# Rows of w and u spread by shuffles, quartered weights and new planner durations in a fused RWKV-5 and feed-forward kernel

## The chip, the cores and the metric

The kernel runs on one core of a Trainium2 chip. The core has a matrix engine (PE, with its weight loads PEld), a vector engine (DVE), a scalar engine (ACT), a general engine (POOL) and a synchronising engine (SP), each with its own in-order instruction queue, and 16 DMA engines which all queues share. The metric is device time in microseconds of one execution.

## The reference

For each of 4 batches and 8 heads (768 steps, head size 48) a state of 48 x 48 is carried along the sequence:

```python
for t in range(S):
    cur = np.einsum('bhd,bhe->bhde', u[None] * kt, vt)
    y[:, :, t] = np.einsum('bhd,bhde->bhe', rt, state + cur)
    state = w[None, :, :, None] * state + np.einsum('bhd,bhe->bhde', kt, vt)
```

Then y, as 3072 tokens of 384, goes through a feed-forward part: `h = x @ w_in` (384 to 2048), an elementwise gate (h above 1, 0 below -1, (h+1)^2/4 between), and `g @ w_out` (2048 to 384). All inputs and the output are float32.

## The kernel before, in words

The sequence is cut in chunks of 128 steps, so the recurrence becomes matrix work. A group g is one chunk of two batches; there are 12 groups of two units (one batch's chunk each), and unit n belongs to group n // 2.

For each group the kernel loads R, K and V (384 KB each) from DRAM by SP's queue (lines 239 and 316). Group 0's R and K come in two halves of 192 KB each, here called R0.0, K0.0, R0.1, K0.1 (the second figure is the batch). R is multiplied by Wup and K by Wdn (powers of w by row, lines 258 and 260), giving Rs and Ks; KU = K u and RKU = R KU (lines 262, 264), a sum of RKU by head (line 289) and V2 = V times that sum (line 294) make the u term. For groups 0 to 4 PE transposes Rs and Ks (T, line 340) and ACT or DVE copies them out (TT, line 163); later groups use DMA transposes (RT, KT, line 424). PE makes A (line 351), DVE masks it (AT, line 356), PE makes the state's update Sp (line 363) and Y (lines 373, 378), DVE adds V2 (y, line 385). The state is multiplied by wCm, a power of w spread over a 96-wide block, on POOL (line 398) or, in the first chunk, on DVE (line 395). y is transposed to xT, on PE for the first three groups (X, line 406), by DMA later (line 447).

The feed-forward part takes 256 tokens of a group in four quarters q: mm1 (12 matmuls to hp, line 463), relu and square on ACT (pt and sq, lines 470 and 474), the gate on DVE (gt, line 478), then mm2 (line 497) for each of the two units, whose result ACT copies out (o_sb) and SP stores. mm1 of q needs its part of w_in, mm2 of q its part of w_out. There are two hp buffers and nine gt buffers.

w and u at the start: both are broadcast over 128 partitions by the transfer (lines 81, 82); ACT makes lw = ln w (line 170), Wup and Wdn by exp (lines 173, 176). w_col holds w by column; POOL squares it seven times (line 180) and ACT spreads it into wCm (line 185).

The order of all work is made when the kernel is built, by a list planner (lines 519 to 581). Each operation is declared with `op(name, where, key, fn, needs, makes, uses)`: the engines it may run on with a duration each, a due time (key), what it needs, which buffers it takes and uses. The planner always takes the engine with the earliest possible start and, on it, the operation with the lowest key among those that can start within 0.25 us, and appends its instructions to that engine's queue. The engines then run these queues in order, with semaphores only where data or buffers demand it. A table SHIFT (line 124) moves the due times of kinds of operations and of single groups.

Weights go by POOL's queue in two halves each (lines 201, 205), which also casts them to bfloat16. Two operations make SP's queue wait: a one-element memset on POOL into R of group 1, behind the w_in issues (line 236), and a small transfer out of w_out's first half ahead of R of group 2 (line 238).

Of the kernel before, what the change touches and what calls it, by code (L numbers as in the profile page):

```python
# [22 lines left out]
def kernel(  # L23
# [51 lines left out]

    w_col = const.tile([P, NP], F32, name="w_col")
    nc.vector.memset(w_col, 1.0)
    mark = const.tile([1, 16], BF16, name="mark")
    w_bc = const.tile([P, DM], F32, name="w_bc")
    u_bc = const.tile([P, DM], F32, name="u_bc")  # L80
# [35 lines left out]

    lw = const.tile([P, DM], F32, name="lw")
# [37 lines left out]

    tiles = {}
# [12 lines left out]
    def lw_ln(e):  # L169
        nc.scalar.activation(lw, w_bc, AF.Ln, bias=0.0)  # L170
# [16 lines left out]
    op("w_bc", (("NET", 0.0, 4.4),), -99, None)  # L187
    op("u_bc", (("NET", 0.0, 5.0),), -99, None)
    op("w_col", (("NET", 0.0, 7.2),), -99, None)
    op("lw", (("ACT", 0.6),), -98, lw_ln, ["w_bc"])  # L190
    op("Wup", (("ACT", 2.0),), -97, wup, ["lw"])
    op("Wdn", (("ACT", 0.7),), -96, wdn, ["Wup"])
    op("w_power", (("POOL", 0.9),), -50, w_power, ["w_col"])
    op("wCm", (("ACT", 0.9),), -49, w_spread, ["w_power"])


    NW = 2
    for i in range(NW):
        def w_in_go(e, i=i):
            n = slice(i * DF // NW, (i + 1) * DF // NW)  # L200
            nc.gpsimd.dma_start(out=w_in_sb[:, :, n], in_=w_in_src[:, :, n])

        def w_out_go(e, i=i):
            n = slice(i * nF // NW, (i + 1) * nF // NW)
            nc.gpsimd.dma_start(out=w_out_sb[:, n, :], in_=w_out_src[:, n, :])

        k_in, k_out = -70 + i, -2 + i * 0.1 + shift("w_out", i)
        op(f"w_in{i}!", (("POOL", 0.8),), k_in, w_in_go, [f"w_in{i - 1}!"] if i else ["load K0.1"])
        op(f"w_in{i}", (("DMA", 4.3, 2.0),), k_in, None, [f"w_in{i}!"])
        op(f"w_out{i}!", (("POOL", 0.9),), k_out, w_out_go, ["load R1.0"])  # L210
        op(f"w_out{i}", (("DMA", 5.0, 2.0),), k_out, None, [f"w_out{i}!"])
# [7 lines left out]
    for g in range(nG):  # L219
# [4 lines left out]
        for j0, j1 in parts:  # L224
# [5 lines left out]
            for i, (x, what) in enumerate(((r, "R"), (k, "K"))):  # L230

                def load(e, g=g, j0=j0, j1=j1, x=x, what=what):
                    if j0 == 0:
                        tiles[what, g] = loads.tile([P, UNITS * H, D], F32, name=what, tag=what)
                    if g == 1 and what == "R":
                        nc.gpsimd.memset(tiles[what, g][:1, 0, :1], 0.0)
                    if g == 2 and what == "R":
                        nc.sync.dma_start(out=mark, in_=w_out_sb[:1, 0, :16])
                    nc.sync.dma_start(out=tiles[what, g][:, j0 * H : j1 * H, :], in_=source(x, g, j0, j1))

                op(f"load {what}{tag}", (("DMA", 1.1 * n, 2.0),), tl + i * 0.3, load, [[], ["w_in1!"], ["w_out0"]][g] if g < 3 else [],
# [24 lines left out]
            pool_or_dve = (("POOL", 0.95 * n), ("DVE", 0.65 * n)) if early_g else (("POOL", 0.92 * n),)  # L266
            pool_only = (("POOL", 0.95 * n),)
            first = j0 == 0
            for i, (what, needs) in enumerate(
# [11 lines left out]
                where = pool_or_dve if i < 2 or g in (1, 2) else pool_only  # L281
                if g == 0 and i < 2:
                    where = (("DVE", 0.6),)
# [240 lines left out]
    free = {"POOL": 4.2, "DVE": 3.0}  # L524
    done = {}
    waiting = dict(ops)
    SLACK, HOP = 0.25, 0.06
    log = []
    last_uses = {}
    queue = {}  # L530
# [81 lines left out]
```

## Time and profile before

| | us |
|---|---|
| median of 3 runs | 192.14 (191.78 to 192.76) |
| the profiled execution | 191.3 |
| its span | 189.5 |
| first mm1 matmul | 22.59 |
| issue of w_in halves on POOL | 10.63 and after |
| issue of w_out halves on POOL | 25.69 and 30.32 |
| issue of R of groups 1 and 2 on SP | 16.62 and 33.57 |

The granted PE clock is full throughout. Busy time of an engine counts its instructions' spans, which overlap on PE; a stretch's columns are PE, PEld, DVE, ACT and POOL busy, each with its number of instructions, the granted clock, the DMA engines' mean busy share (which can come out over 1, as packets overlap) and GB/s. In a row of the timeline the first number is the start, the second the duration, and in brackets the idle time of that engine before it and what ended it. In the chain the two numbers are start and duration. In the rows of the DMA queues they are packets, MB and the share of 16 engines' span.

### The profile page before, as it was taken

The page shows a single profiled execution, that of the slowest core. Times are in us where ns is not written, and L with a number is a line of the kernel's source. Part 1 is how long each engine was busy: PE and PEld are TensorE (multiplying, and loading weights), DVE is VectorE, ACT ScalarE, POOL GpSimd, SP SyncE. Part 2 cuts the span into 40 slices and gives each one's busy share as a digit, 9 for nine tenths or more (in the row PEclk, how much of TensorE's full clock was granted, in tenths as well). Part 3 has the DMA queues.
Part 4 walks back from the last instruction along what each step waited for, and adds up shares of the span by engine and source line. Part 5 has one row for each costly group of instructions (what it writes and reads, how often), then busy time and mean ns, then how long its engine had stood idle before and what let it go on. Part 6 is the DMA issues. An engine that isn't in the chain of part 4 may idle for free.

```text
span 189.5 us, 4017 instructions
## 1 busy us (share of the span) xinstructions
PE 160.8 (85%) x1602; PEld 117.8 (62%) x1602; DVE 135.8 (72%) x181; ACT 134.8 (71%) x166; POOL 118.2 (62%) x95
## 2 busy tenths in 40 slices
PE   0214676599979899989999999999999999999992
PEld 0113454467857677667677677677777767777750
DVE  3477419964989999986969869787888876654540
ACT  3334367938856699986898888869798786778741
POOL 5294095029799999999997999799897300000000
PEclk9999999999999999999999999999999999999999
DMA  4979989979997299899997999799798221121112
GB/s 99 167 117 182 223 136 166 189 150 192 226 249 155 70 186 201 174 194 207 173 218 153 206 182 196 162 177 214 151 197 151 66 66 21 42 66 42 42 42 83
DMA packets 103346, 28.11 MB, mean 148 GB/s; under 512 B 97184, under 2 KB 102560, under 8 KB 103328
## 3 DMA queue, kind: packets, MB, share of 16 engines
q1 hardware_dynamic: 100096, 24.32, 62.7%
q0 software_dynamic: 2944, 3.15, 11.1%
q10 hardware_dynamic: 288, 0.39, 1.0%
q8 instruction: 12, 0.20, 0.4%
q14 instruction: 6, 0.05, 0.1%
HBM read 20.84 MB, written 4.72 MB: 135 GB/s over the span
## 4 chain that ended last, share of the span: by engine, by line
PE 55%; POOL 16%; DVE 8%; DMA 7%; ACT 6%; issue 4%; SPq 0%; POOLq 0%
PE op L497 25%; PE hp L463 24%; POOL KU L262 4%; DMA K<-in_k_dram 4%; POOL RKU L264 3%; POOL Ks L260 3%; DVE gt L478 3%; PE A L351 3%; POOL V L294 2%; DMA KT<-Ks 2%; ACT pt L470 2%; DVE AT L356 2%; ACT sq L474 2%; POOL Rs L258 2%; DMA xT<-y 1%
## 5 line engine op out<-in xcount | busy, mean ns | idle before, releaser
L478 DVE SCALAR_TENSOR_TENSOR gt<-sq,hp 128x1024 bf16<-128x1024 f32 x48 | 58.5, 1218 | 28.4 <-ACT sq L474 28.3
L463 PE MATMUL hp<-xT,w_in_sb 128*128 128x256 bf16 x576 | 72.2, 277 | 3.9 <-DVE gt L478 2.3
L497 PE MATMUL op<-w_out_sb,gt 128*128 128x384 bf16 x384 | 71.0, 326 | 1.6 <-DVE gt L478 0.7
L470 ACT ACTIVATE pt<-hp 128x1024 f32<-128x1024 f32 x48 | 49.1, 1023 | 26.2 <-PE hp L463 25.8
L463 PEld LDWEIGHTS <-w_in_sb 128*128 128x128 bf16 x576 | 56.9, 99 | 16.3 <-issue 4.1
L474 ACT ACTIVATE sq<-pt 128x1024 f32<-128x1024 f32 x48 | 50.8, 1058 | 1.2
L497 PEld LDWEIGHTS <-gt 128*128 128x128 bf16 x384 | 34.5, 97 | 22.2 <-issue 1.3
L356 DVE TENSOR_TENSOR AT<-A,umask 128x512 bf16<-128x512 f32 x48 | 30.8, 683 | 2.5 <-PE A L351 2.1
L258 POOL TENSOR_TENSOR Rs<-R,Wup 128x768 bf16<-128x768 f32 x11 | 20.1, 1828 | 17.6 <-DMA R<-in_r_dram 17.6
L262 POOL TENSOR_TENSOR KU<-K,u_bc 128x768 f32<-128x768 f32 (+1 forms) x13 | 23.3, 1790 | 4.2 <-DMA K<-in_k_dram 4.2
L264 POOL TENSOR_TENSOR RKU<-R,KU 128x768 f32<-128x768 f32 (+1 forms) x13 | 22.5, 1732 | 0.5
L398 POOL TENSOR_TENSOR state<-Tm,wCm 128x384 f32<-128x384 f32 x16 | 16.2, 1014 | 2.5 <-DVE Tm L393 2.4
L294 POOL TENSOR_TENSOR V<-V,diag 128x768 f32<-128x768 bf16 x10 | 14.8, 1483 | 4.7 <-DVE diag L289 3.3
L260 POOL TENSOR_TENSOR Ks<-K,Wdn 128x768 bf16<-128x768 f32 x9 | 16.5, 1829 | 0.0
L385 DVE TENSOR_TENSOR y<-Y,V 128x384 bf16<-128x384 f32 x24 | 13.3, 555 | 4.3 <-PE Y L378 3.0
L163 ACT CAST V<-VF 128x768 bf16<-128x768 f32 x12 | 9.9, 828 | 5.6 <-DMA VF<-in_v_dram 5.6
L378 PE MATMUL Y<-V,AT 128*128 128x48 bf16 x192 | 11.9, 186 | 1.9 <-DVE AT L356 1.9
L163 ACT COPY o_sb<-op 128x384 f32<-128x384 f32 x22 | 10.2, 468 | 3.6 <-PE op L497 3.5
L163 ACT CAST state_bf<-state 128x384 bf16<-128x384 f32 x20 | 10.1, 504 | 3.4 <-DVE state L395 2.8
L289 DVE TENSOR_REDUCE diag<-RKU 128x16 f32<-128x768 f32 (+1 forms) x13 | 11.5, 883 | 1.3 <-POOL RKU L264 1.3
L378 PEld LDWEIGHTS <-AT 128*128 128x128 bf16 x192 | 9.8, 98 | 2.9 <-DVE AT L356 2.6
L340 PE MATMUL T<-ident,Rs 128*128 128x128 bf16 x40 | 4.3, 237 | 6.8 <-DVE Rs L258 6.5
(50 smaller groups left out, 106.7 us busy)
## 6 DMA issues: line engine op xcount, KB each, us to landing
VF<-in_v_dram SPq DMA_DIRECT2D x12, 384.0 KB, 4.3
out_dram<-o_sb SPq DMA_DIRECT2D x24, 192.0 KB, 2.3
R<-in_r_dram SPq DMA_DIRECT2D x11, 384.0 KB, 4.6
K<-in_k_dram SPq DMA_DIRECT2D x11, 384.0 KB, 5.9
w_in_sb<-in_moe_w_in_dram POOLq DMA_DIRECT2D x2, 768.0 KB, 9.0
w_out_sb<-in_moe_w_out_dram POOLq DMA_DIRECT2D x2, 768.0 KB, 8.4
R<-in_r_dram SPq DMA_DIRECT2D x2, 192.0 KB, 5.9
K<-in_k_dram SPq DMA_DIRECT2D x2, 192.0 KB, 5.8
```

What stands on the lines that cost most here:

```text
L163: nc.scalar.copy(out, in_) if e == "ACT" else engines[e].tensor_copy(out, in_)
L258: engines[e].tensor_mul(part(R_s)[:, :, :, :D], part(R), rep(Wup, j1 - j0))
L260: engines[e].tensor_mul(part(K_s)[:, :, :, :D], part(K), rep(Wdn, j1 - j0))
L262: engines[e].tensor_mul(part(tiles["KU", g]), part(K), rep(u_row, j1 - j0))
L264: engines[e].tensor_mul(part(tiles["RKU", g]), part(R), part(tiles["KU", g]))
L356: nc.vector.tensor_mul(tiles["AT", n][:, i], tiles["A", n][i], umask.unsqueeze(1).to_broadcast([P, NP, P]))
L378: nc.tensor.matmul(Y[:, 2 * p + i, :], AT[:, i, p, :], V[:, j * H + 2 * p + i, :], start=(c == 0), stop=True, skip_group_check=True,)
L463: nc.tensor.matmul(hp[:, f, :], w_in_sb[:, i, n0 : n0 + P], tiles["xT", g][:, i, :], start=(i == 0), stop=(i == nK - 1), skip_group_check= ...
L470: nc.scalar.activation(tiles["pt", g, q], tiles["hp", g, q], AF.Relu, bias=0.5, scale=0.5)
L474: nc.scalar.activation(tiles["sq", g, q], tiles.pop(("pt", g, q)), AF.Square, bias=0.0)
L478: nc.vector.scalar_tensor_tensor(out=gt, in0=tiles.pop(("sq", g, q)), scalar=1.0, in1=tiles.pop(("hp", g, q)), op0=ALU.min, op1=ALU.max)
L497: nc.tensor.matmul(tiles["op", g, j], tiles["gt", g, q][:, f, j * P : (j + 1) * P], w_out_sb[:, n, :], start=(n == 0), stop=(n == nF - 1),)
```

## The change

- w and u are loaded as four rows each (partitions 0, 32, 64, 96) into tiles set to 1 and 0 before; a shuffle within each 32 partitions on DVE spreads ln w and u.
- The scalar table is loaded as a set with ln alone at the start and as one with exp behind ln.
- w_col comes by ACT's queue; its squarings may be put on DVE.
- Weights go in four quarters each. Quarter 0 of w_in is issued by POOL behind a one-element copy which reads R0.1, quarter 2 behind one of K of group 1; quarter 0 and 2 of w_out behind R and K of group 2.
- The memset into R and the small transfer out of w_out are gone. In the planner, loads of R of groups 1, 2 and 3 are placed after w_in's quarter 1, its quarter 3 and w_out's quarter 3.
- T of the first four units no longer needs A of the unit before.
- Durations in the planner are new, most with a latency of their own; products on POOL and DVE exclude each other in it (PORT); an operation with two possible engines is entered once, with the one that ends first; KU and RKU of group 0 may go to DVE.

```diff
-    nc.scalar.dma_start(out=w_bc, in_=bcast(w))
-    nc.scalar.dma_start(out=u_bc, in_=bcast(u))
+    nc.vector.memset(w_row, 1.0)
+    nc.vector.memset(u_row4, 0.0)
+    nc.scalar.dma_start(out=w_row[0:P:QUAD, :], in_=bcast(w, P // QUAD))
+    nc.scalar.dma_start(out=u_row4[0:P:QUAD, :], in_=bcast(u, P // QUAD))
+    nc.scalar.preload_act_table_set("natural_log")
     for j in range(2):
-        nc.gpsimd.dma_start(out=w_col[j * HP : j * HP + D, :], in_=src)
-    nc.scalar.preload_act_table_set("natural_log_exp_and_others")
+        nc.scalar.dma_start(out=w_col[j * HP : j * HP + D, :], in_=src)
...
+    LOAD_AFTER = {("R", 1): ["w_in1"], ("R", 2): ["w_in3"], ("R", 3): ["w_out3"]}
...
+    def lw_spread(e):
+        nc.vector.stream_shuffle(lw, lw_row, [0] * QUAD)
+    def u_spread(e):
+        nc.vector.stream_shuffle(u_bc, u_row4, [0] * QUAD)
...
+    op("exps", (("ACT", 1.28),), -98, lambda e: nc.scalar.preload_act_table_set("exp_and_others"), ["lw_row"])
-    op("w_power", (("POOL", 0.9),), -50, w_power, ["w_col"])
+    op("w_power", (("DVE", 0.6),), -50, w_power, ["w_col"])
...
-    NW = 2
+    NW = 4
+    GATE_IN = {0: ("R", 0, 1), 2: ("K", 1, 1)}
+    GATE_OUT = {0: ("R", 2, 1), 2: ("K", 2, 1)}
+        def gate_on(what, g, j):
+            x = tiles[what, g][:1, (j + 1) * H - 1, :1]
+            nc.gpsimd.tensor_copy(gone[:1, :1], x)
...
-                    if g == 1 and what == "R":
-                        nc.gpsimd.memset(tiles[what, g][:1, 0, :1], 0.0)
-                    if g == 2 and what == "R":
-                        nc.sync.dma_start(out=mark, in_=w_out_sb[:1, 0, :16])
...
-                op(f"T{n}", (("PE", 0.46),), ka, t_in, [f"Rs{part}", f"Ks{part}"] + ([f"A{n - 1}"] if n else []), ...
+                op(f"T{n}", (("PE", 0.45, 0.17),), ka, t_in, [f"Rs{part}", f"Ks{part}"] + ([f"A{n - 1}"] if n > 3 else []), ...
-            op(f"relu {m}", (("ACT", 1.13),), k1 + 0.2, relu, ...
+            op(f"relu {m}", (("ACT", 0.93, 0.1),), k1 + 0.2, relu, ...
...
+            best = None
             for w in where:
-                s = max([start, free.get(e, 0.0)] + [done[x][0] + (HOP if done[x][1] != e else 0.0) for x in needs])
-                found.append((s, key, len(found), name, w))
+                s = max([start, free.get(e, 0.0)] + [free.get(x, 0.0) for x in w[3:]] + [done[x][0] + HOP[e] if done[x][1] != e else done[x][2 if e == "DMA" else 0] for x in needs])
+                if best is None or s + w[1] < best[0] + best[4][1]:
+                    best = (s, key, len(found), name, w)
+            found.append(best)
```

More of the change, by code (lines that the diff above doesn't have):

```diff
@@ L204, in w_out_go, with after @@
             n = slice(i * nF // NW, (i + 1) * nF // NW)
+            if i in GATE_OUT:
+                gate_on(*GATE_OUT[i])
             nc.gpsimd.dma_start(out=w_out_sb[:, n, :], in_=w_out_src[:, n, :])
[L207 to L211, printed above, removed]
+        def after(gates, i, prev):
+            need = [f"{prev}{i - 1}!"] if i else []
+            if i in gates:
+                what, g, j = gates[i]
+                need.append(f"load {what}{g}.{j if g == 0 else 0}")
+            return need
+        k_in = -70 + i if i < 2 else -12 + i * 0.1
+        k_out = -1 + i * 0.1 + shift("w_out", i)
+        op(f"w_in{i}!", (("POOL", 0.5, 1.2),), k_in, w_in_go, after(GATE_IN, i, "w_in"), [], [GATE_IN[i][:2]] if i in GATE_IN else [])
+        op(f"w_in{i}", (("DMA", 2.05, 1.3),), k_in, None, [f"w_in{i}!"])
+        op(f"w_out{i}!", (("POOL", 0.55, 1.2),), k_out, w_out_go, after(GATE_OUT, i, "w_out"), [], [GATE_OUT[i][:2]] if i in GATE_OUT else [])
+        op(f"w_out{i}", (("DMA", 1.95, 1.3),), k_out, None, [f"w_out{i}!"])
     def turned(n, i, p):
@@ L523 @@
     left = dict(users)
-    free = {"POOL": 4.2, "DVE": 3.0}
+    free = {"POOL": 3.9, "DVE": 3.0, "DMA": 2.5}
     done = {}
     waiting = dict(ops)
-    SLACK, HOP = 0.25, 0.06
+    SLACK, HOP = 0.25, {"PE": 0.06, "POOL": 0.08, "ACT": 0.04, "DVE": 0.04, "DMA": 0.1, "NET": 0.0}
     log = []
```

92 lines of the change are left out of this document (50 added, 42 removed).

## The prediction

> **What bounds the kernel now.** I read the page's busy times, then the stretches, then the chain that ended last, then the timeline of the first 50 us and the DMA queues.
>
> ```profile
> PE 160.8 (85%) x1602; PEld 117.8 (62%) x1602; DVE 135.8 (72%) x181; ACT 134.8 (71%) x166; POOL 118.2 (62%) x95
> q1 hardware_dynamic: 100096, 24.32, 62.7%
> q0 software_dynamic: 2944, 3.15, 11.1%
> q10 hardware_dynamic: 288, 0.39, 1.0%
> ```
>
> PE is the busiest engine, but not evenly. Stretches (first pair of numbers: PE busy; at the end the DMA share):
>
> ```profile
> 10.00:20.00 10.00, 4.13 (x44) 2.98 (x44) 7.12 (x11) 4.44 (x7) 6.02 (x13) 1.00 0.93 152
> 30.00:35.00 5.00, 3.20 (x39) 2.29 (x36) 4.72 (x6) 3.96 (x5) 1.26 (x2) 1.00 1.12 161
> 35.00:40.00 5.00, 3.04 (x43) 2.03 (x44) 5.00 (x8) 3.18 (x4) 0.00 (x0) 1.00 0.97 163
> 50.00:55.00 5.00, 4.27 (x56) 3.13 (x54) 4.30 (x8) 4.37 (x6) 4.32 (x3) 1.00 1.21 223
> 90.00:100.00 10.00, 10.00 (x99) 7.13 (x98) 7.82 (x11) 9.04 (x13) 9.97 (x7) 1.00 1.07 191
> ```
>
> From 90 us PE is full; only 0.72 us of its idle time lies between 90 and 180. What can be won lies before. Idle PE from the first feed-forward matmul at 22.59 to 40 is about 5.5 us, from 40 to 90 another 2.7. The chain and the timeline name two causes:
>
> ```profile
> 15.82 0.21 POOL w_col L180
> 16.61 0.35 ACT wCm L163
> 17.35 1.02 ACT TT L163
> 19.07 1.29 DVE AT L356 x2
> 22.06 0.49 ACT xT L163
> 22.59 2.73 PE hp L463 x12
> ```
>
> ```profile
> 11.49 0.83 ACT L163 CAST V<-VF 128x768 bf16<-128x768 f32 x1 [5.28 <-DMA VF<-in_v_dram]
> 12.23 1.01 ACT L163 COPY TT<-T 128x1024 bf16<-128x1024 bf16 x1
> 23.95 1.80 POOL L258 TENSOR_TENSOR Rs<-R,Wup 128x768 bf16<-128x768 f32 x1 [7.36 <-DMA R<-in_r_dram]
> 41.46 1.80 POOL L258 TENSOR_TENSOR Rs<-R,Wup 128x768 bf16<-128x768 f32 x1 [10.20 <-DMA R<-in_r_dram]
> 43.17 0.96 DVE L260 TENSOR_TENSOR Ks<-K,Wdn 128x768 bf16<-128x768 f32 x1 [2.16 <-DMA K<-in_k_dram]
> ```
>
> First, in-order ACT: unit 0's TT stands behind the V cast, unit 1's TT behind wCm, which waits for seven tiny squarings on POOL behind its products. Second, POOL stands 7.36 and 10.20 us for R of groups 1 and 2. That is DMA capacity: 62.7% of 189.5 us over 100096 packets, times 2048 packets of 192 B, is 2.43 us of all 16 engines for one 384 KB load; 11.1% is 21.0 us for the four weight halves, 5.26 each; 1.0% is 1.9 us for the broadcasts of w and u. Up to K of group 2 that is 8 x 2.43 + 21.0 + 1.9 = 42.3 us, and begun near 2 us it ends at 44.3; K of group 2 was there by 43.17. So the DMA engines are full from the start to 43 us, and only the order of the traffic and the 1.9 us can change.
>
> **The change part by part.**
>
> *Broadcasts gone.* -1.9 us of DMA ahead of the row loads. K0.0 arrived at 7.95; without this, near 6.2.
>
> *The w path.* Two 128x384 memsets on DVE (the same shape took 0.38 in wCm) stand before the two small transfers on the ACT queue: +0.5 on their issue, then less to move, so Ln starts about 4.4 as before (4.54). Then comes a second table load, which the row of the first prices at 1.28; the shuffle lies beside it. No row shows a shuffle; DVE rows of 128x384 f32 bound it between 0.38 (memset) and 0.56 (product), I take 0.5, near the product, which also reads and writes SBUF. The one of w lies beside the load; the one of u falls in the 3.24 us for which DVE waited before Rs of group 0. Ln to 4.95, load to 6.3, Wup 6.9, Wdn 7.45 (before 5.70 and 6.22). K0.0 now waits for Wdn instead of DMA: Ks0.0 starts at 7.5 instead of 8.01, -0.5. The Trainium skill speaks against this step (ScalarE: Activation LUTs, "Table sets: the hidden batching unit"): ln and exp share one set, so one load would do, and a switch costs 2.66 us with its drain. By that Ks0.0 would start at 8.9, AT of unit 1 (below) would end by 16.9, and the old 2.24 from there to the first feed-forward matmul give 19.1 instead of 18.9 and a sum of 188.6. The trace of before can't tell: ACT waited 1.58 us for w behind its only load, which would hide a drain.
>
> *w_power to DVE, w_col to the ACT queue.* POOL loses 7 squarings (2.11 us) and two issues (1.36); DVE gets seven, between 0.06 (the smallest DVE row) and 0.2 (POOL's median) each, about 0.7. Unit 1's TT no longer waits for 16.5, nor its T for A of unit 0: TT of both units near 9 to 11.5, AT to 14.5 or 15.5 (four of 0.64 plus sums and V2 at 0.55 each on DVE, with products of group 0 that now may go there).
>
> *What is late next: V of group 0.* SP no longer waits (marks and memset gone; the new list of load-after names orders the planner only). It issues R0, K0, V0, R1, K1, V1, R2, K2 back to back, and POOL starts w_in quarters 0 and 1 as soon as R0.1 has landed, near 7, flowing from 8. How rows and weights share: R1 was issued at 16.62 while the second w_in half (issued near 11.4, 10.6 to landing, so 22.0) was moving, and landed at 23.95; of its 2.43 us 1.95 came after 22.0. So weights take about 88%. Two quarters, 5.26 / 0.88 = 6.0, hold the engines from 8 to 14; V0, of which about 1.5 is left at 8, lands between 10 (if weights start late) and 15.2 (before: 11.45). I take 15.2, as the row argues. V cast 16.1, V2 17.2, then the old tail from there (y 0.55, X 0.6, xT 0.5, hops): first feed-forward matmul at 18.9 instead of 22.59, -3.7; bounds 17.3 and 20.5.
>
> *Group 1 and the gates.* R1 lands at 17.6, K1 at 20.0 (before 23.95, about 26.6). The gate on K1 blocks POOL, but what is behind it, KU of group 1, needs K1 too; behind the gates on R2 and K2 stand Rs and KU of group 2, which need these loads as well. Quarters 2 and 3: from 21.3 to 27.3. V1 27.6, y and xT of group 1 near 31.5 (before 41.64). R2 lands at 30 and opens w_out quarters 0 and 1 (31 to 37); K2, held up by them, near 38 and opens quarters 2 and 3 (39 to 45.3). Eight issues of half size at 0.4 to 0.8 are 3.2 to 6.4 (before four, 3.46); four gate copies, priced between POOL's 0.09 memset and 0.2 squaring, add 0.4 to 0.8. All in POOL's former idle 17 us: nothing.
>
> *What this is worth.* mm2 of group 0 needs the last w_out quarter: 45.3 plus 1.3, so it ends near 47, and before it ended at 47.06 (the op run from 44.47). The earlier start is therefore not kept in full: at 47 us PE is ahead by what it could do instead, the second half of mm1 of group 1 (2 x 1.31) and the T, A and Sp of group 2 (about 1.2), together 3.8. Group 3's rows come at 48 to 53, as before (Rs of group 3 began at 47.66), but POOL then has group 2 behind it and does V2 earlier (was 60.17 to 61.65), so mm1 of group 3, before at 71.75, moves by about the same 3.7. From there PE is full: the lead stays.
>
> *Planner's durations.* They redo the order everywhere; the table of shifts stays. In the second half the gain is at most the 0.72 of idle PE there; the loss is bounded by the density of the stretch from 50 to 90, 2.6 idle in 40, which over 90 us is 5.9. I take 0, the value of the rows from 90 on, since lengths of 1.03 and 1.06 for ACT agree with the new figures.
>
> Sum: 191.3 (span 189.5 plus 1.8 around it) - 3.7 = 187.6 for a profiled execution. The median of the runs, 192.14, stands 0.84 above the profiled one, so the forecast for a median is 188.4. Half a per cent, about 1 us, is what a measurement here can tell from no change.
>
> **The rivals.**
>
> *B, the lead grows* to about 7 us: if weights yield more to rows than 88%, K2 comes near 34 and the last w_out quarter near 41, and mm1 of group 2 starts 7 to 9 us before its 57.90. For: group 1 is ready 10 us earlier. Against: traffic to 43 us is the same. 191.3 - 7 + 0.8 = 185.1, reaching to 183.
>
> *C, slower by the new order.* Shifts chosen beside the old durations are kept, so in-order engines may meet gaps in the second half as dense as from 50 to 90: 188.4 + 5.9 = 194.3. It decides from 4.7 us of new idle, where it is over half a per cent slower. For: from 90 to 140 DVE and ACT are 0.77 to 0.90 busy and POOL 0.83 to 1.00, and the old plan's lengths (1.13 against 1.02 measured for pt) left slack. Against: a list that never leaves PE idle with work ready, with true lengths.
>
> *D, w_out too late.* PE takes its work in the planned order; if K2 lands after 43 instead of 38, the last quarter comes after 50 instead of 45.3 and PE stands at mm2 of group 0. The lead of 3.8 is gone at 49.1; at 53 the time is 192.1 + 3.9 = 196.0. For: two gates in a row, each behind a load that weights slow. Against: the sum of traffic ends by 45.
>
> *E, no effect:* group 3 binds, since R3 cannot land before 48; its products (4 x 1.82 on POOL) start as before and PE waits the lead away: 191.5 to 192.5.
>
> **How the numbers follow.** Forecast 0.40, B 0.23, C 0.18, D 0.10, E 0.09. Forecast and B, with a little of C, are faster: 0.65. E and the edge of C: 0.09. C and D: 0.26. The forecast's own range is 186.5 to 190.0 (start bounds 17.3 and 20.5). The range leaves out the ends of B and D and the outer half of C: 183.5 to 194.3.
>
> **What would show it.** First feed-forward matmul at 17.3 to 20.5; two table loads and Wup near 6.9; V cast near 15 to 16; the idle of POOL before Rs of groups 1 and 2 (7.36 and 10.20) mostly gone; w_out's last landing near 45; mm2 of group 0 ending near 47; mm1 of group 3 near 68. I am wrong if PE idles over 4 us after 90, if the last w_out lands after 49, or if V0 lands by 11 and PE starts before 17.

## The result, and the profile after

The changed kernel has a median of 200.01 us (198.80 to 200.95); the kernel before, run on the same chip beside it, 192.45 (191.78 to 193.55). The ratio is 1.038, with a 95% interval of 1.030 to 1.047: slower by some 7.6 us, where I had forecast 3.7 us gained. The profiled execution of after took 198.8 us, with a span of 197.0 (before 191.3 and 189.5). An execution more than 1.5% longer than the fastest of the same kernel counts as slow: here and below a median is over all executions, a ratio and its interval leave the slow ones out.

The page of after: busy times, PE and its clock in 40 slices of 4.9 us each, two of the DMA queues, and one of its issue rows (KB each, median us from issue to landing).

```profile
PE 164.2 (83%) x1602; PEld 119.2 (61%) x1602; DVE 141.5 (72%) x205; ACT 134.6 (68%) x167; POOL 101.4 (51%) x82
...
PE   0064768299889989999694799999999999999992
...
PEclk9999999579999999999999799999999999999998
...
q1 hardware_dynamic: 100064, 24.32, 68.8%
...
q10 hardware_dynamic: 432, 0.01, 0.2%
...
VF<-in_v_dram SPq DMA_DIRECT2D x12, 384.0 KB, 5.9
```

PE has the same 1602 matmuls, but two dents (the 2 in slice 8, the 4 in slice 22), and in them or right behind them PEclk falls below 9 (slices 8, 9 and 23). The broadcasts' 1.0% of the DMA engines has become 0.2%. Work has moved from POOL (118.2 to 101.4) to DVE (135.8 to 141.5). The same dents in the stretches of after:

```profile
10.00:20.00 10.00, 5.65 (x59) 3.73 (x59) 9.83 (x19) 4.26 (x6) 1.72 (x3) 1.00 1.32 197
...
35.00:40.00 5.00, 1.80 (x6) 0.86 (x6) 4.86 (x7) 0.88 (x2) 0.93 (x1) 0.54 1.15 187
...
90.00:100.00 10.00, 8.18 (x81) 5.73 (x78) 6.75 (x10) 8.02 (x10) 8.52 (x6) 1.00 0.91 170
100.00:110.00 10.00, 6.10 (x65) 4.36 (x63) 4.16 (x7) 4.83 (x6) 5.48 (x4) 1.00 1.10 189
110.00:120.00 10.00, 10.00 (x89) 6.78 (x87) 7.90 (x12) 7.21 (x11) 7.93 (x6) 0.83 0.99 174
```

and, for the two stretches not shown yet, of before:

```profile
100.00:110.00 10.00, 9.72 (x104) 7.38 (x103) 8.54 (x12) 8.49 (x11) 8.28 (x7) 1.00 0.93 188
110.00:120.00 10.00, 10.00 (x101) 7.38 (x100) 8.39 (x11) 8.51 (x12) 9.55 (x7) 1.00 0.93 186
```

From 90 to 110 PE of after was busy 14.28 us, that of before 19.72. In the stretch after that it is busy throughout but does 89 matmuls for 101, at a granted clock of 0.83.

To see where the time was lost I took, from the timeline's ACT rows, the start of the first relu of each group. It dates the feed-forward part group by group:

| us | group 0 | 1 | 2 | 3 | 4 | 5 | last relu | span |
|---|---|---|---|---|---|---|---|---|
| before | 25.34 | 43.19 | 59.41 | 73.26 | 86.06 | 98.46 | 179.96 | 189.5 |
| after | 24.02 | 46.77 | 61.91 | 73.73 | 87.16 | 106.25 | 186.50 | 197.0 |
| difference | -1.3 | +3.6 | +2.5 | +0.5 | +1.1 | +7.8 | +6.5 | +7.5 |

A lead of 1.3 becomes a loss of 3.6 by group 1, and nearly all of that is made good by group 3, where PE of before still had idle time to catch up in. Between groups 4 and 5 another 6.7 us are lost, and by group 6 (119.50, before 111.20) 7.2; PE of before is full there and after, so little of it comes back. After the last relu come 10.5 us instead of 9.5: about 1 us more at the end.

**The first hole.** Timeline of after, 31 to 41 us (start, duration; in brackets the idle time before and its end):

```profile
31.22 0.95 DVE L287 TENSOR_TENSOR Rs<-R,Wup 128x768 bf16<-128x768 f32 x1
...
33.56 0.95 DVE L291 TENSOR_TENSOR KU<-K,u_bc 128x768 f32<-128x768 f32 x1
...
33.70 0.40 PE L369 MATMUL T<-ident,Ks 128*128 128x128 bf16 x4
...
34.10 1.06 ACT L503 ACTIVATE sq<-pt 128x1024 f32<-128x1024 f32 x1
...
35.53 0.95 DVE L318 TENSOR_REDUCE diag<-RKU 128x16 f32<-128x768 f32 x1
36.59 0.96 DVE L323 TENSOR_TENSOR V<-V,diag 128x768 f32<-128x768 bf16 x1
37.47 0.68 DVE L169 COPY TT<-T 128x1024 bf16<-128x1024 bf16 x1
38.07 1.21 DVE L507 SCALAR_TENSOR_TENSOR gt<-sq,hp 128x1024 bf16<-128x1024 f32 x1
38.20 2.72 PE L526 MATMUL op<-w_out_sb,gt 128*128 128x384 bf16 x8 [4.11 <-DVE TT L169]
```

PE has finished T (34.10) and ACT the square (35.16). What both need next is DVE: the copy TT and the gate. In DVE's queue group 2's products, sum and V2 stand before them, though PE takes group 2's T only at 44.81. POOL, which made most of group 2's products in the kernel before, stands idle meanwhile, from 31.2 to 39.07, for R of group 3.

**The second hole.** The same view, 90 to 110 us:

```profile
91.44 0.83 ACT L169 CAST V<-VF 128x768 bf16<-128x768 f32 x1 [2.17 <-DMA VF<-in_v_dram]
...
92.83 4.02 SPq L453 DMA_TRANSPOSE RT<-Rs  x1
...
95.59 1.47 PE L492 MATMUL hp<-xT,w_in_sb 128*128 128x256 bf16 x12 [1.82 <-DVE gt L507]
...
99.11 0.46 ACT L169 COPY o_sb<-op 128x384 f32<-128x384 f32 x1
...
100.43 0.56 SPq L345 DMA_DIRECT2D VF<-in_v_dram  x1
...
105.10 0.83 ACT L169 CAST V<-VF 128x768 bf16<-128x768 f32 x1 [5.53 <-DMA VF<-in_v_dram]
...
108.39 1.22 DVE L507 SCALAR_TENSOR_TENSOR gt<-sq,hp 128x1024 bf16<-128x1024 f32 x1 [5.84 <-ACT sq L503]
...
109.66 1.98 PE L492 MATMUL hp<-xT,w_in_sb 128*128 128x256 bf16 x12 [3.90 <-DVE gt L507]
```

A V is issued at 100.43 and lands 4.65 us later; ACT comes to its cast 5.53 us too early and stands there. Behind the cast in ACT's queue is the relu, behind that the square, the gate, and the hp buffer that mm1 needs. The planner now counts 1.8 + 1.35 = 3.15 us from the start of a V's issue to its landing. It used to count 4.2, and the issue row of before shows that this was what V took:

```profile
VF<-in_v_dram SPq DMA_DIRECT2D x12, 384.0 KB, 4.3
```

(In before the V issued at 97.57 was cast at 103.88, with no wait.) The shortest of the twelve landings in after took 4.2 us, so the new figure was never reached. But the latency is the smaller part of this wait. ACT was done with o_sb at 99.57, 0.86 us before the load was even issued: SP's queue is in order too, and in it V stood behind transposes and a store, among them RT, whose issue alone took 4.02 us (the planner has 1.4). Landing 3.15 us after its issue, V would still have kept ACT for 4.0 of the 5.53 us. In all, ACT waited 14.2 us in seven V casts (before 5.6 in two).

**The clock.** Both holes bring matmuls at half the granted clock: from 35.38 to 42.20 and from 110.48 to 113.89. The eight mm2 matmuls at 38.20 took 2.72 us, where the eight at 116.13 took 1.46. The second spell, all of it with a full PE, costs half of 3.41, 1.7 us. With the 5.4 us by which PE idled more from 90 to 110 it makes 7.1, about the 7.2 that are lost by group 6. (A first spell alone does not set after apart: g1, below, has one too, with a clock of 0.78 from 30 to 40.)

### The profile page after: what moved, and what is told of

It is laid out like the page before. It is cut to its first block, busy times and chain, and to the rows that moved or that the text cites. A ratio compares the mean times of both kernels' runs of the same rounds, so it can differ in the third digit from the quotient of the medians.

```text
span 197.0 us, 4036 instructions
## 1 busy us (share of the span) xinstructions
PE 164.2 (83%) x1602; PEld 119.2 (61%) x1602; DVE 141.5 (72%) x205; ACT 134.6 (68%) x167; POOL 101.4 (51%) x82
## 3 DMA queue, kind: packets, MB, share of 16 engines
q0 software_dynamic: 3712, 3.15, 9.9%
## 4 chain that ended last, share of the span: by engine, by line
PE 48%; DMA 16%; DVE 13%; ACT 10%; POOL 5%; issue 4%; SPq 2%; POOLq 0%; DVEq 0%; ACTq 0%
PE op L526 21%; PE hp L492 21%; DMA VF<-in_v_dram 14%; ACT sq L503 4%; ACT pt L499 4%; DVE gt L507 3%; DVE AT L385 2%; PE A L380 2%; DMA R<-in_r_dram 2%; DVE Rs L287 1%; PE Y L407 1%; ACT state_bf L169 1%; ACT V L169 1%; POOL state L427 1%; DVE RKU L293 1%
## 5 line engine op out<-in xcount | busy, mean ns | idle before, releaser
L492 PE MATMUL hp<-xT,w_in_sb 128*128 128x256 bf16 x576 | 73.0, 278 | 9.4 <-DVE gt L507 8.7
L526 PE MATMUL op<-w_out_sb,gt 128*128 128x384 bf16 x384 | 75.6, 334 | 4.9 <-DVE TT L169 4.1
L526 PEld LDWEIGHTS <-gt 128*128 128x128 bf16 x384 | 35.1, 99 | 25.8 <-issue 6.9
L287 POOL TENSOR_TENSOR Rs<-R,Wup 128x768 bf16<-128x768 f32 x9 | 16.4, 1821 | 7.9 <-DMA R<-in_r_dram 7.9
L169 ACT CAST V<-VF 128x768 bf16<-128x768 f32 x12 | 10.0, 833 | 14.2 <-DMA VF<-in_v_dram 14.2
L293 POOL TENSOR_TENSOR RKU<-R,KU 128x768 f32<-128x768 f32 x9 | 16.3, 1816 | 0.4
L291 POOL TENSOR_TENSOR KU<-K,u_bc 128x768 f32<-128x768 f32 x9 | 16.4, 1823 | 0.0
L323 POOL TENSOR_TENSOR V<-V,diag 128x768 f32<-128x768 bf16 x9 | 13.3, 1477 | 4.7 <-DVE y L414 2.7
```

Source lines behind the costliest of these rows:

```text
L169: nc.scalar.copy(out, in_) if e == "ACT" else engines[e].tensor_copy(out, in_)
L287: engines[e].tensor_mul(part(R_s)[:, :, :, :D], part(R), rep(Wup, j1 - j0))
L293: engines[e].tensor_mul(part(tiles["RKU", g]), part(R), part(tiles["KU", g]))
L492: nc.tensor.matmul(hp[:, f, :], w_in_sb[:, i, n0 : n0 + P], tiles["xT", g][:, i, :], start=(i == 0), stop=(i == nK - 1), skip_group_check= ...
L526: nc.tensor.matmul(tiles["op", g, j], tiles["gt", g, q][:, f, j * P : (j + 1) * P], w_out_sb[:, n, :], start=(n == 0), stop=(n == nF - 1),)
```

## The experiments

The runs are grouped by question, not in the order in which they were made. In the quoted texts theory 1 is that the new load durations are too short, 3b that the old durations give good orders in general, 8 that the products of group 2 come too early. "Ratio" is against the kernel before, beside the same runs, with its 95% interval.

### Transfers or order?

`f1`: the kernel before, its order untouched, with w and u as rows, shuffles, two table sets, w_col on ACT's queue.

```diff
-    nc.scalar.dma_start(out=w_bc, in_=bcast(w))
-    nc.scalar.dma_start(out=u_bc, in_=bcast(u))
+    nc.scalar.dma_start(out=w_row[0:P:QUAD, :], in_=bcast(w, P // QUAD))
+    nc.scalar.dma_start(out=u_row4[0:P:QUAD, :], in_=bcast(u, P // QUAD))
...
+        nc.vector.stream_shuffle(lw, lw_row, [0] * QUAD)
+        nc.vector.stream_shuffle(u_bc, u_row4, [0] * QUAD)
+        nc.scalar.preload_act_table_set("exp_and_others")
```

> The kernel before, its order kept on every engine, with the new loading of w and u alone: rows and shuffles, two table loads, w_col by ACT's queue (squarings stay on POOL). Theory 3: the new front gains by 1.9 us less DMA: 189.5 to 191 against 191.2. Theory 4: the second table load delays all that follows: 192 or more.

188.10 us, ratio 0.988 (0.984 to 0.992): faster. The first mm1 starts at 21.00 (before 22.59), group 1's relu at 41.29 (43.19), the last relu at 176.25 (179.96). This part of the change is worth 1.2%.

`f2`: f1 without the two things that made SP wait.

```diff
-                    if g == 1 and what == "R":
-                        nc.gpsimd.memset(tiles[what, g][:1, 0, :1], 0.0)
-                    if g == 2 and what == "R":
-                        nc.sync.dma_start(out=mark, in_=w_out_sb[:1, 0, :16])
```

> The run before this one with the two waits of SP taken out as well (the memset into R of group 1 and the small transfer out of w_out), weights still in halves, order kept. Theory 3: R of groups 1 and 2 arrive by 17 and 32 instead of 23.95 and 41.4, and the time is 186 to 190. Theory 4: rows and weights hold each other up, and the time is 193 or more.

190.02 us, ratio 0.997 (0.993 to 1.001): between the two forecasts. R of group 1 is multiplied at 14.79 instead of 22.04, and yet 1.0% is lost. Relu of group 1 starts 0.7 us later than in f1, that of group 4 2.2 later. Why the earlier row loads cost time with this order was not followed further.

`g1`: f2 with all of the new weight traffic, quarters and four gates, but still the order of before on PE, DVE and ACT.

```diff
+            if i == 0:
+                gate_on("R", 0, 1)
+                w_in_quarters(0, 2)
...
+            if i == 0:
+                gate_on("K", 1, 1)
+                w_in_quarters(2, 4)
+            else:
+                for what, x in (("R", r), ("K", k)):
+                    tiles[what, 2] = loads.tile([P, UNITS * H, D], F32, name=what, tag=what)
+                    nc.sync.dma_start(out=tiles[what, 2], in_=source(x, 2, 0, UNITS))
+                gate_on("R", 2, 1)
+                w_out_quarters(0, 2)
+                gate_on("K", 2, 1)
+                w_out_quarters(2, 4)
```

> All transfers of the change (rows and shuffles, no wait on SP, weights in quarters, the four gates on R0.1, K of group 1, R and K of group 2) in the order that the kernel before has on PE, DVE and ACT; on POOL the second pair of w_in goes behind Rs of group 1, and both pairs of w_out behind RKU of group 1. Squarings stay on POOL. Theory 7 (the order alone is at fault): 187 to 191. Theory 6 (the transfers cost): 195 or more.

191.14 us, ratio 0.999 (0.995 to 1.004). Stretches of g1:

```profile
90.00:100.00 10.00, 10.00 (x104) 7.19 (x102) 7.60 (x11) 9.07 (x12) 10.00 (x8) 1.00 1.08 184
100.00:110.00 10.00, 10.00 (x106) 7.49 (x105) 9.06 (x13) 8.81 (x12) 8.67 (x6) 1.00 1.03 193
```

With all the transfers of after, PE is full where after had its second hole, and the time is that of before. So the loss of 3.8% lies in what g1 leaves out of the change, the new order (which instruction stands where in each queue, and on which engine; SP's order of loads from V of group 2 on is part of it). Against f1, the transfers that g1 adds cost about what f1 gains. The other half of the test is the new planner alone.

`p1`: the kernel before, with all new durations and the new rule of choice (and what else is new in the planner: T without A, group 0's KU and RKU on DVE too), and its own transfers.

```diff
-                op(f"load {what}{tag}", (("DMA", 1.1 * n, 2.0),), ...
+                op(f"load {what}{tag}", (("DMA", 0.9 * n, 1.35),), ...
...
-            op(f"relu {m}", (("ACT", 1.13),), ...
+            op(f"relu {m}", (("ACT", 0.93, 0.1),), ...
...
+                if best is None or s + w[1] < best[0] + best[4][1]:
+                    best = (s, key, len(found), name, w)
+            found.append(best)
```

> The kernel before with its own transfers, waits and tables, but with all durations and the choice rule of the changed planner. Theory 3 (the new order of the work costs, whatever the transfers are; the table of shifts fits the old durations): 196 to 202. Theory 4 (what costs is in the transfers: no wait on SP, quarters and gates, rows and shuffles): within 1.5 us of before.

210.61 us, ratio 1.106 (1.101 to 1.112), the slowest of all. Two rows of p1's timeline:

```profile
31.45 0.96 DVE L258 TENSOR_TENSOR Rs<-R,Wup 128x768 bf16<-128x768 f32 x1 [12.22 <-DMA R<-in_r_dram]
...
33.59 2.72 PE L463 MATMUL hp<-xT,w_in_sb 128*128 128x256 bf16 x12 [8.98 <-DVE gt L478]
```

It is the mechanism of after's first hole, larger: DVE has come to Rs of group 1, whose load the planner thought long there, and stands 12.22 us; a gate stands behind it, and PE behind the gate. The new planner fares better with the new transfers, in which rows come earlier (1.038), and even with them it loses.

`n1`: the kernel before with one small change to the planner, to see whether its good order is one lucky fit.

```diff
-    SLACK, HOP = 0.25, 0.06
+    SLACK, HOP = 0.25, 0.07
```

> The kernel before with one number of its planner moved by a hundredth of a microsecond (the hop between engines 0.07 instead of 0.06), which makes no duration truer. Theory 3a (the old order is a single fit, and nearly any other order costs several us): 193 to 198. Theory 3b (an order made by the old durations is good in general, and the new durations are at fault): within 1 us of before.

190.67 us, ratio 1.001 (0.997 to 1.005). Shaking the old planner does not bring the loss: one shake only, but it speaks against the lucky fit.

### Which of the durations?

`e3`: the kernel before with nothing new but the durations of the loads.

```diff
-                op(f"load {what}{tag}", (("DMA", 1.1 * n, 2.0),), ...
+                op(f"load {what}{tag}", (("DMA", 0.9 * n, 1.35),), ...
-            op(f"loadV{g}", (("DMA", 2.2, 2.0),), ...
+            op(f"loadV{g}", (("DMA", 1.8, 1.35),), ...
```

> The kernel before, with only the planner's durations of the row loads of the change (0.9 per half, 1.8, 1.35). Theory 1: V casts come too early in ACT's order here too, ACT waits over 10 us before them and the time is 195 to 199. Theory 2 and theory 3: within 1 us of before.

200.15 us, ratio 1.038 (1.031 to 1.045). Waits of e3 (total us, times, longest):

```profile
ACT V L163 <- DMA VF<-in_v_dram: 15.1, 3, 12.9
```

The load figures alone cost as much on the old kernel as the whole change, though at another place: V of group 0 is planned early, lands late, a TT stands behind its cast, and PE waits 11.73 us for that TT.

`e1`: the changed kernel with the old load durations back (the two lines of e3, reversed).

> The changed kernel, with the planner's durations of the row loads alone put back (R and K 1.1 per half and 2.0 to landing, V 2.2 and 2.0; in the change 0.9, 1.8 and 1.35). Theory 1 (V loads land later than the planner believes, and ACT, in order, stands before V casts, 14.2 us in the changed kernel): the waits before V casts fall under 6 us, the hole between 90 and 110 us is gone, and the time is 192 to 194. Theory 2 (DVE is overfull with the products of groups 1 and 2): the hole near 35 to 38 us stays and so does most of the time, 197 to 200. Theory 3 (the whole new order is poor, at many places): 196 or more.

197.23 us, ratio 1.032 (1.025 to 1.039). A PE row of e1's timeline:

```profile
43.52 3.82 PE L526 MATMUL op<-w_out_sb,gt 128*128 128x384 bf16 x12 [4.81 <-DVE TT L169]
```

V casts wait 4.1 us in all instead of 14.2, and PE is busy for all of 90 to 110. But group 1 now starts at 52.34, 5.6 later than in after, behind DVE's products again, and there is a new hole of 2.21 us before 127.63. Theory 1 names the cause of the second hole, not of the loss.

`e2`: the changed kernel with a longer latency for V alone.

```diff
-            op(f"loadV{g}", (("DMA", 1.8, 1.35),), ...
+            op(f"loadV{g}", (("DMA", 1.8, 2.85),), ...
```

> The changed kernel, with one number changed: the planner's time from the end of a V load to its use is 2.85 instead of 1.35, the 4.65 from issue to landing that the load before the longest wait took. SP's order stays that of the changed kernel beyond the first groups; only ACT's order changes, with V casts later. Theory 1: waits before V casts fall under 5 us, 192 to 195. Theory 2 and theory 3: 197 or more.

200.10 us, ratio 1.037 (1.029 to 1.045). No gain: V casts still wait 9.8 us, and PE has two new holes, 2.98 us before 115.30 (for the DMA of xT) and 3.05 before 130.90 (for a gate). (The profile is that of the longest of four executions, 201.44 us; the shortest took 197.32, so these holes need not be in all.)

### Which rule?

`p2`: the changed kernel's transfers with all old durations and the old rule; only loads follow one another by the end of their issue, as in after. `q1`: p2 with the new rule of choice, with products on POOL and DVE excluding each other, and with group 0's KU and RKU on DVE too.

```diff
-            pool_or_dve = (("POOL", 0.95 * n), ("DVE", 0.65 * n)) if early_g else (("POOL", 0.92 * n),)
+            pool_or_dve = (("POOL", 0.95 * n, 0.0, "PORT"), ("DVE", 0.65 * n, 0.0, "PORT")) if early_g else (("POOL", 0.92 * n, 0.0, "PORT"),)
...
-                found.append((s, key, len(found), name, w))
+                if best is None or s + w[1] < best[0] + best[4][1]:
+                    best = (s, key, len(found), name, w)
+            found.append(best)
...
-        free[e] = s + cost
+        for x in (e, *w[3:]):
+            free[x] = s + cost
```

> The changed kernel with its own rows, shuffles, quarters and gates and no wait on SP, but with the durations and the choice rule of the planner before. Theory 5 (only the new durations and the new choice cost, the transfers are sound): 187 to 193. Theory 6 (the transfers cost too, since gates and waits were what kept rows and weights apart): 195 or more.

> The run before this one, with the new choice rule put back (an operation entered once, with the engine that ends first; POOL and DVE products exclude each other in the planner; KU and RKU of group 0 may go to DVE), durations still those of before. If the choice is at fault: over 3 us above the run before this one. If the durations are: within 2 us of it.

p2: 199.33 us, ratio 1.046 (1.039 to 1.054). q1: 195.21, ratio 1.024 (1.018 to 1.030). p2's time is the one that the quoted text gives for theory 6, but g1 has the same transfers at 0.999, so p2's loss too lies in its order. q1 is the faster by 4.1 us, against both of its forecasts: the new rule, with the two things that came with it, is a gain of 2% under the old durations. The old durations in place of the new ones are worth some 1.4% under the new rule (1.024 to 1.038; the intervals just meet). But the old durations, which give a good order with the old transfers, give a poor one with the new. q1 has caught up with before by group 4 (relu at 85.83, before 86.06) and is level up to group 7 (123.57, before 124.21). Then one V cast puts it 3.3 us behind (group 8 at 139.95, before 136.61), and 3.3 is what its span has over that of before (192.8). This V was issued at 127.27, ACT was ready for it at 128.91, and it landed 5.51 us after its issue; the planner of q1 counts 4.2, so here too more of the wait (2.6 of 3.86 us) comes of a late issue than of a latency put too short. Timeline of q1:

```profile
132.78 0.83 ACT L169 CAST V<-VF 128x768 bf16<-128x768 f32 x1 [3.86 <-DMA VF<-in_v_dram]
...
137.19 2.72 PE L492 MATMUL hp<-xT,w_in_sb 128*128 128x256 bf16 x12 [2.76 <-DVE gt L507]
```

### Can single repairs save the new order?

`e4`: the changed kernel with products of groups 1 and 2 on POOL alone. `g2`: e4 and e1 together.

```diff
-                where = pool_or_dve if i < 2 or g in (0, 1, 2) else pool_only
+                where = pool_or_dve if g == 0 else pool_only
```

> The changed kernel, with the products of groups 1 and 2 offered to POOL alone, not to DVE (group 0 as in the change). Theory 2: the 4.1 us for which PE waits near 38 for DVE's TT goes, relu of group 1 starts by 44 instead of 46.77, and the time falls by 3 to 6 us, to 194 to 197. Theory 1: the hole between 90 and 110 stays; what is won in front is lost there, 198 to 201.

> The changed kernel with both single repairs together: the planner's old durations of row loads, and products of groups 1 and 2 on POOL alone. If the two misplacements (DVE overfull near 35 us, V casts ahead of their loads near 100) are all that costs: 189 to 193. If the repairs make new holes elsewhere, as each did alone: 196 or more.

e4: 201.29 us, ratio 1.042 (1.034 to 1.050). The first hole is gone: group 1's relu is at 44.03, group 2's at 57.24, before that of the kernel before (59.41). But PE idles at other places, 1.66 us before 107.02 and 3.19 before 129.43; timeline of e4:

```profile
125.02 0.83 ACT L169 CAST V<-VF 128x768 bf16<-128x768 f32 x1 [4.94 <-DMA VF<-in_v_dram]
...
129.43 1.47 PE L492 MATMUL hp<-xT,w_in_sb 128*128 128x256 bf16 x12 [3.19 <-DVE gt L507]
```

g2: 200.04 us, ratio 1.044 (1.037 to 1.051). Two repairs, each of which removes the hole it aims at, do not add up: PE now waits for X at 34.95 and 39.34 (1.69 and 1.60 us), for Y at 75.99 and for a gate at 143.52.

`h1`: e1, with R of group 2 planned behind w_out's second quarter, and w_out gated on R of group 1 alone. `h2`: the same two lines on q1.

```diff
-    LOAD_AFTER = {("R", 1): ["w_in1"], ("R", 2): ["w_in3"], ("R", 3): ["w_out3"]}
+    LOAD_AFTER = {("R", 1): ["w_in1"], ("R", 2): ["w_out1"], ("R", 3): ["w_out3"]}
...
-    GATE_OUT = {0: ("R", 2, 1), 2: ("K", 2, 1)}
+    GATE_OUT = {0: ("R", 1, 1)}
```

> The changed kernel with the old durations of row loads (197.2 alone) and with R of group 2 planned behind w_out's second quarter, as before, and w_out gated on R of group 1 instead of R and K of group 2. Theory 8: DVE's hole for PE near 35 to 43 us is gone, relu of group 1 starts by 45, and the time falls by 3 us or more, to 190 to 194. Otherwise: 196 or more.

> The run with all old durations, the new choice rule and the new transfers (195.2), with R of group 2 planned behind w_out's second quarter and w_out gated on R of group 1. Theory 8: relu of group 1 starts by 45 instead of 49.6, and the time is 189 to 192.5. Otherwise: 194.5 or more.

h1: 197.73 us, ratio 1.025 (1.019 to 1.031). h2: 194.74, ratio 1.019 (1.013 to 1.026). In h1 group 1 is early (relu 40.62), but group 2 late (66.67, before 59.41), and there is a gate wait at 148 (its profile is that of the longest of six executions, 199.84 us; the shortest took 195.71). In h2 it is w_in that comes late:

```profile
33.53 2.74 PE L492 MATMUL hp<-xT,w_in_sb 128*128 128x256 bf16 x12 [6.64 <-DMA w_in_sb<-in_moe_w_in_dram]
```

Theory 8 names what makes the first hole; taking it away moves the hole to the next group or to the weights.

### What the two table sets and the squarings cost

`f3`: f1 with one table set for ln and exp. `f4`: f3 with the squarings of w_col on DVE.

```diff
-    nc.scalar.preload_act_table_set("natural_log")
+    nc.scalar.preload_act_table_set("natural_log_exp_and_others")
-        nc.scalar.preload_act_table_set("exp_and_others")
...
-            engines[e].tensor_mul(w_col, w_col, w_col)
+            nc.vector.tensor_mul(w_col, w_col, w_col)
```

> The kernel before in its own order with the new loading of w and u, but with one table set that holds ln and exp, so without the second table load of 1.28 us. Wup then starts when the shuffle ends, about 5.55 instead of 6.21. If the second load lies on the path: 0.4 to 0.8 below the run with two loads, 187.3 to 187.7. If other work covers it: the same 188.1 within 0.3.

> The run before this one, with the seven squarings of w_col on DVE, as the change has them; all other work in the order of before. wCm is then done about 2 us earlier and unit 1's TT, which stands behind it on ACT (15.77 with the squarings on POOL), starts near 13.5. If this is what holds the first feed-forward matmul: it starts at 19 to 19.8 instead of 21.0 and the time is 185.5 to 187. If the rows of group 2 decide: within 0.5 us of the run before this one.

f3: 188.01 us, ratio 0.988 (0.982 to 0.993), no different from f1. Wup starts at 5.87 instead of 6.21, but the first mm1 at 21.03 instead of 21.00. The second load is covered. f4: 188.71, ratio 0.988 (0.981 to 0.994); its first mm1 starts at 20.84. That is neither the start of 19 to 19.8 nor, by 0.2 us, the half microsecond that the quoted text left for the other case; squarings on DVE instead of POOL neither help nor harm by more than these intervals.

## Why the prediction was wrong, point by point

**The step that failed is "Planner's durations ... I take 0".** It costed the redone order at nothing, with bounds of 0.72 gained and 5.9 lost. Measured on the spans, the order took 6.9 us (after 197.0, g1 190.1). The lead of 3.7 failed beside it: in the old order all the transfers together bring nothing (g1, 0.999), since what the rows of w and u gain (f1) the rest takes back. The first of my signs of being wrong, PE idle for over 4 us after 90, was there: 5.7 us from 90 to 110. I argued that lengths of 1.03 and 1.06 for ACT agree with the new figures. They do, and ACT's own rows agree with them still, but the step never looked at the other new figures: the row loads, where 3.15 us stood against a median of 4.3 in a row of the page of before. That row was there to be read. Nor did it ask what a list of operations with two engines does when DVE is put at 1.01 us for a product and POOL at 1.78, and the one that ends first is entered: the products of groups 1 and 2 went to DVE, the engine of the gates and of TT. These two are what makes the holes of after; they are not shown to be the whole reason of the loss. p2 has none of the new durations for engines and loads of rows, nor the new rule, and loses 4.6%; q1 has the rule and gains on p2; e4 takes the products off DVE and gains nothing. What the runs show is that the order made anew for these transfers costs, by the old durations as by the new.

**Rival C had the mechanism** (in-order engines meet gaps in the new order), but bounded it by the density of 50 to 90. It happened in two places. The one that it named, the second half, gave 7.2 us between groups 4 and 6, with two V casts: PE idle 1.82 before 95.59 and 3.90 before 109.66, and the half clock after that. About 1 us more came at the end. What C held against itself, a list that never leaves PE idle with work ready, holds only inside the planner's own clock: it has the load issued and landed before it is.

**First mm1 at 18.9 (17.3 to 20.5): 21.27.** The w path came out nearly as worked out. Timeline of after:

```profile
5.63 0.57 DVE L179 STREAM_SHUFFLE lw<-lw_row 128x384 f32<-128x384 f32 x1
...
6.91 0.61 ACT L185 ACTIVATE Wup<-lw,up_col 128x384 f32<-128x384 f32 x1
...
8.84 0.55 DVE L291 TENSOR_TENSOR KU<-K,u_bc 128x384 f32<-128x384 f32 x1
...
9.30 0.55 DVE L287 TENSOR_TENSOR Rs<-R,Wup 128x384 bf16<-128x384 f32 x1
...
18.73 0.94 DVE L287 TENSOR_TENSOR Rs<-R,Wup 128x768 bf16<-128x768 f32 x1
...
19.60 0.55 DVE L414 TENSOR_TENSOR y<-Y,V 128x384 bf16<-128x384 f32 x1
...
21.27 2.72 PE L492 MATMUL hp<-xT,w_in_sb 128*128 128x256 bf16 x12 [0.57 <-ACT xT L169]
```

The second load (1.28 us) begins at 5.61 and the shuffle lies beside it; that took 0.57, at the upper of my bounds. Wup starts at 6.91, where I had its end at 6.9: 0.6 us late, since ln began at 5.07 and not near 4.4. V0 was not late: SP issued it at 3.91, and by the chain it landed 4.93 us later, at 8.84, while w_in's first quarters were issued from 6.19 to 7.9. My 15.2 charged it with two quarters of weights; the lower bound of 10 was already too high. What was late in its place is DVE: 9.83 of the 10 us from 10 to 20 busy. The squarings (1.34 us, I had 0.7), before which DVE stood 0.88 us for w_col, and KU stood before Rs and Ks of unit 0; Ks, which I had at 7.5, started at 9.77. Rs of group 1 stood before y of unit 1 (18.73, 19.60). I had named those products as something that "now may go there" and put no time to it.

By the page "ScalarE: Activation LUTs" of the Trainium skill (section "Table sets: the hidden batching unit") the second load is a cost, since one set holds ln and exp. f3 saves it and gains nothing (188.01 against 188.10), because Rs of unit 0 is not what the end waits for. The 2.66 us for a switch with its drain, which the same page of the Trainium skill gives in its section "What ACT_TABLE_LOAD costs", is not what this trace shows: Wup starts 0.02 us after the end of the 1.28.

**Group 1 and the gates.** Timeline of after, the last three of POOL's four gate copies:

```profile
17.46 0.17 POOL L218 COPY gone<-K 1x1 f32<-1x1 f32 x1 [9.56 <-DMA K<-in_k_dram]
...
21.46 0.46 POOL L218 COPY gone<-R 1x1 f32<-1x1 f32 x1 [2.01 <-DMA R<-in_r_dram]
...
29.24 0.17 POOL L218 COPY gone<-K 1x1 f32<-1x1 f32 x1 [5.81 <-DMA K<-in_k_dram]
```

All of these loads came earlier than forecast: K1 at 17.46 (20.0), R2 at 21.46 (30), K2 at 29.24 (38). The xT of group 1, forecast near 31.5, did not: its first unit's copy started at 32.66, its second's at 43.28, after the TT that DVE reached at 37.47. The 88% that I read from one R behind a weight half (0.48 of its 2.43 us in the 5.4 up to 22.0 is rather 91%) did not hold here, where several row loads and two quarters were in flight together. So rival D, w_out too late, is out: its last quarters were issued by 31.2, not after 39. Rival B had the reason for these early loads right and drew the wrong end from it: the early groups 1 and 2 became DVE's burden. The copies took 0.97 us (I had 0.4 to 0.8) and the eight issues 6.3, all in time in which POOL had nothing else, as I had it; but POOL's idle time is not gone, it has moved into the gates (9.56, 2.01, 5.81, and then 7.90 for R of group 3). I had said that it would be mostly gone. R3, which rival E put at 48 at the earliest, was multiplied at 39.07, so E's premise was wrong too; and yet group 3 came no earlier (relu 73.73, before 73.26), where I had its mm1 3.7 us earlier.

**Broadcasts gone, -1.9 us of DMA:** right in size (1.0% to 0.2% of the queues' row), and f1, which holds this and the w path, is worth 1.2%. The mechanism that I gave for it shows in f1's trace: KU of unit 0 no longer waits for its load and starts at 6.38 instead of 8.06, and the first mm1 is as much earlier, 1.6 us. f2 shows that the second half of my gain, row loads without SP's waits, is a loss of 1.0% against f1 where the order stays.

**What stays open:** why the old durations with the new transfers (p2, q1) give a worse order than with the old ones. Each of e1, e2, e4, g2, h1 and h2 removes or moves the hole that it aims at, and another appears. Part of the reason is that SP's queue comes to a load later than the plan has it (the V casts of after and of q1 above), which a longer latency in the plan did not mend (e2); why SP falls behind so far was not followed. The table of shifts was left as it was in all of them. That it fits the old order, and that a new one would repair this, is a guess that was not tried.

## What to carry to other kernels

Change the transfers and the order apart from each other: f1, with the order kept, is the best version here with f3, which is no different (188.10 us, 1.2% faster than before), and the whole change hid that gain behind a net loss of three times its size. In a planner's list, lengths of engine work may be exact, but a load's latency has to be the one that the full DMA engines give (for V at the least 4.2 us here, 5.9 in the median, not 3.15). That alone is not enough (e2): the queue that issues the loads is in order too, and when it comes to one late, the engine that waits for it stops, with all that stands behind it. And when an operation may run on two engines, ask which queue it would stand in front of before asking where it ends first.

## What the runs showed of the hardware that I had not expected

A hole in PE's work can cost more than its length, and need not be long. In after the granted clock changes only at times that lie multiples of 3.41 us apart (35.38, 42.20, 110.48, 113.89). Stretches of after cut on that grid, and below them one of q1's, where the clock falls at about 136.6:

```profile
31.97:35.38 3.41, 1.77 (x20) 1.21 (x18) 3.38 (x5) 3.38 (x5) 0.00 (x0) 1.00 1.34 209
...
93.41:96.82 3.41, 1.59 (x15) 1.20 (x13) 2.42 (x3) 3.38 (x5) 3.33 (x3) 1.00 1.02 155
...
103.66:107.07 3.41, 2.10 (x26) 1.36 (x25) 0.00 (x0) 1.97 (x3) 1.82 (x2) 1.00 1.34 215
107.07:110.48 3.41, 0.82 (x8) 0.73 (x8) 2.09 (x4) 3.35 (x5) 0.00 (x0) 1.00 1.03 186
110.48:113.89 3.41, 3.41 (x21) 1.83 (x20) 2.86 (x5) 1.60 (x4) 3.21 (x3) 0.50 1.21 214
```

```profile
133.15:136.55 3.40, 1.29 (x8) 0.67 (x7) 0.84 (x2) 3.40 (x5) 3.32 (x4) 1.00 0.68 157
```

Windows with PE busy for 0.82, 1.29 and 1.77 us are followed by half the clock, those with 1.59 and 2.10 are not. So the busy time of this view settles it only outside a band: in the eighteen traces here, each cut on its own grid from 26 us on, every window at full clock with PE busy for 1.52 us or less is followed by half, none with 1.86 or more is, and between the two both happen. It isn't the length of the hole that decides: q1's of 2.76 us brought the half clock, and e4's of 3.19 and p2's of 2.75 did not. The Trainium skill ("TensorE: Matmul & The Clock Gate", "Part 1: The HAM clock gate") states the free-running window of 3413 ns and the two levels, 4/8 and 8/8, and the trace agrees with both. For the fall it names an idle window, though, or (section "HAM oscillation — how this bites in real kernels") a gap of more than some 3.4 us; here a window that was still half busy (1.77 of 3.41) was enough. At the front the clock's row may not show the state: the first twelve mm1 matmuls took 2.72 us there too, against 1.47 later, at a shown clock of 1.00.

Products on DVE and POOL at the same time slow each other: in p1, from 45.4 to 53 us, three products take 2.44 to 2.58 us each on DVE, and of three on POOL beside them the first keeps its 1.80 and the others take 2.48 and 2.51, where alone a product takes 0.95 and 1.81. The three pairs together take 7.6 us; one after the other they would have taken 8.3, so little is won. The new planner excludes this in its plan; in p1 it happened on the chip all the same.
